# Norm 1's statistics moved to TensorE from a transposed load, and the far lag table made in two halves

## Chip, cores and metric

One core of one Trainium2 chip. The metric is the device time of one execution in microseconds (us), over several executions. Engines: TensorE (PE), VectorE (DVE), ScalarE (ACT), GpSimd (POOL), SyncE (SP, which here only issues transfers).

## The reference, cut to what matters

```python
x = A_u                                                  # 2048 tokens x 512 channels, bf16
h  = x + _A_ref(_layernorm(x), A_re, ..., Dskip)         # "norm 1", then a long convolution over the tokens
h2 = h + _B_ref(_layernorm(h), w1, b1, w2, b2)           # "norm 2", then an MLP over the tokens

def _layernorm(x, axis=-1, eps=1e-5):
    m = jnp.mean(x, axis=axis, keepdims=True)
    v = jnp.var(x, axis=axis, keepdims=True)
    return (x - m) / jnp.sqrt(v + eps)
# _A_ref: K[d,l] = Re sum_n C B dt exp(dt A l);  y = irfft(rfft(u) * rfft(K)) + u * Dskip
# _B_ref: y = gelu(h^T w1 + b1) w2 + b2, transposed back    (w1: 2048 x 1792, w2: 1792 x 2048)
```

## The kernel before

The tokens are 16 blocks of 128. Within a block the convolution is a 128-point transform (`UF`, times the kernel's spectrum `kf`, back through `inv1`, `inv2`). What reaches from earlier blocks goes through "moments" `ms` of the blocks, a shifted copy of them through a scratch in DRAM (`Mb`), a far lag table `G`, and small products `O`. The first half of the tokens (`hf` 0) needs the same as the second (1). The finished blocks `X` are normed (`H`) and multiplied with W1; columns of W1 are either accumulated while the blocks come out, or done afterwards in pairs by a seven-product (Strassen-like) scheme.

```python
    def ln1(self, hf):                                   # statistics of norm 1
        for k in range(lo, hi):
            if k < hi - na:                              # NA = (0, 4)
                b.bn(self.st1[:, k, :], self.X[:, k, :])                               # DVE
            else:                                                                       # ACT
                b.act(self.junk[:, :], self.X[:, k], AF.Copy, accum_out=self.s1[:, 0, k:k + 1])
                b.act(self.cb[:, 0], self.X[:, k], AF.Square, accum_out=self.s1[:, 1, k:k + 1])
        # ... small steps to rs = 1/sigma; Fs = dft * rs; WL = lwin * rs   (cut)
    def shifted(self, hf):                               # ms -> DRAM -> Mb
        self.msw.append(b.dma(self.msd.ap()[120 + 64 * hf:184 + 64 * hf, :], self.ms[64 * hf:64 * hf + 64, :], eng=eng))
        src = bass.AP(tensor=self.msd, offset=64 * hf * D, ap=[[D, P], [8 * D, 8], [1, D]])
        b.dma(self.Mb[:, 8 * hf:8 * hf + 8], src, eng=eng, after=self.msw)
    def lag(self, hf):                                   # far products, 128 per half
        # ... b.mm(self.ps[32 * q:32 * q + 32, 32 * s:32 * s + 32], Gv[:, q, s], Mv[:, q, s])   (cut)
    def y_chunk(self, k):                                # one block out
        # per four blocks, on DVE: Pb = UF * kf(0), UF = UF * kf(1)
        mm(self.bank(yb), self.tb("inv1"), self.Pb[:, t % 2, q], start=True, stop=False)
        mm(self.bank(yb), self.tb("inv2"), self.UF[:, k], start=False, stop=False)
        for f in range(4):                               # the far part
            mm(..., self.tb("lrep", P * f, P), self.O[:, k]...)                         # (cut)
        b.stt(self.X[:, k], self.bank(yb), 1.0, self.X[:, k], ALU.mult, ALU.add, accum_out=self.s2[:, 0, k:k + 1])
    def rest(self):
        first = {0: 3, 1: 6, 2: 7}                       # W1 columns accumulated as blocks come out
        second = {3: 0, 4: 1, 5: 2}                      # (six in all; four pairs by seven products after)
```

A list scheduler sets each engine's order at build time from modelled durations and priorities. A last pass keeps PE warm: wherever its model has PE idle, it fills the gap with products of a constant tile, `ps<-idf`.

```python
    def fill(self):
            # t: when PE is free by the model; start[i]: when the next real product starts by the model
            unit, part = (215.0, 0.92) if cold else (111.0, 0.88)        # ns, share of the gap
            if free and start[i] > t + 60:
                for _ in range(int(part * (start[i] - t - 60) / unit)):
                    ...                                                   # one warming product
```

## Time and profile before

| | before |
|---|---|
| time, median of 2 runs | 156.07 us (155.69 to 156.46) |
| profiled span, granted clock | 154.7 us, 1.000 |
| PE / DVE / ACT busy | 143.5 / 131.4 / 78.2 us |
| last product for `T` (kernel samples) starts on DVE | 34.36 us |
| first lag products (first half of tokens) start | 44.57 us |
| second lag products start (called T_M) | 54.44 us |

Windows: busy time of PE, PEld, DVE, ACT and POOL (with the instructions), the granted clock, the DMA share and GB/s.

```profile
44.57:54.44 9.87, 8.36 (x169) 5.57 (x169) 9.59 (x21) 8.08 (x21) 0.00 (x0) 1.00 0.51 175
54.44:152.40 97.96, 97.55 (x896) 75.13 (x900) 83.02 (x204) 29.86 (x85) 0.00 (x0) 1.00 0.26 96
```

DVE works 9.59 of the 9.87 us before T_M. From T_M to PE's end PE is idle 0.41 us.

### The profile page before, as it was taken

The page shows a single profiled execution, that of the slowest core. Times are in us where ns is not written, and L with a number is a line of the kernel's source. Part 1 is how long each engine was busy: PE and PEld are TensorE (multiplying, and loading weights), DVE is VectorE, ACT ScalarE, POOL GpSimd, SP SyncE. Part 2 cuts the span into 40 slices and gives each one's busy share as a digit, 9 for nine tenths or more (in the row PEclk, how much of TensorE's full clock was granted, in tenths as well). Part 3 has the DMA queues.
Part 4 walks back from the last instruction along what each step waited for, and adds up shares of the span by engine and source line. Part 5 has one row for each costly group of instructions (what it writes and reads, how often), then busy time and mean ns, then how long its engine had stood idle before and what let it go on. Part 6 is the DMA issues. An engine that isn't in the chain of part 4 may idle for free.

```text
span 154.7 us, 3685 instructions
## 1 busy us (share of the span) xinstructions
PE 143.5 (93%) x1522; PEld 106.7 (69%) x1529; DVE 131.4 (85%) x308; ACT 78.2 (51%) x192; POOL 6.7 (4%) x11
## 2 busy tenths in 40 slices
PE   7849869989998889999999999999999999999993
PEld 3738753568565485545554788888888888888882
DVE  5099999998999998999999999957999994558663
ACT  4897999998997868614544832545320000000000
POOL 1590000000000000000000000000000000000000
PEclk9999999999999999999999999999999999999999
DMA  4899996266992508995590000000000101211123
GB/s 108 264 310 360 406 403 240 65 230 176 417 372 83 202 4 310 419 408 222 166 375 3 0 6 0 0 0 4 0 0 0 38 34 68 71 54 51 66 73 103
DMA packets 12351, 23.64 MB, mean 153 GB/s; under 512 B 1181, under 2 KB 8350, under 8 KB 12206
## 3 DMA queue, kind: packets, MB, share of 16 engines
q1 hardware_dynamic: 12190, 23.27, 41.8%
q8 instruction: 12, 0.20, 0.5%
q10 hardware_dynamic: 144, 0.13, 0.2%
q14 instruction: 5, 0.04, 0.1%
HBM read 21.17 MB, written 2.35 MB: 152 GB/s over the span
## 4 chain that ended last, share of the span: by engine, by line
PE 67%; DMA 14%; DVE 7%; SPq 5%; ACT 3%; issue 2%
PE ps L499 67%; DMA tab<-tables 8%; SPq L556 5%; DMA Mb<-ms_scratch 4%; DVE T L522 3%; DVE cmu L522 3%; DMA ms_scratch<-ms 2%; ACT G L506 1%; DVE ct L522 1%; ACT UF L506 1%; PE ps L784 1%; ACT ms L506 0%; ACT kf L506 0%; DVE X L536 0%; ACT mb L506 0%
## 5 line engine op out<-in xcount | busy, mean ns | idle before, releaser
L499 PE MATMUL ps<-H,W 128*128 128x512 bf16 (+1 forms) x180 | 32.5, 327 | 0.3 <-issue 0.2
L499 PEld LDWEIGHTS ps<-H,W 128*128 128x128 bf16 x184 | 17.7, 98 | 10.6 <-DVE H L532 0.2
L784 PE MATMUL ps<-idf 128*128 128x256 bf16 x162 | 22.0, 282 | 1.0 <-POOL idf L547 1.0
L499 PE MATMUL ps<-gT,W 128*128 128x256 bf16 x182 | 22.6, 273 | 0.0
L499 PEld LDWEIGHTS ps<-gT,W 128*128 128x128 bf16 x182 | 17.0, 98 | 3.0 <-DVE X L522 0.2
L784 PEld LDWEIGHTS ps<-idf 128*128 128x128 bf16 x162 | 15.6, 101 | 4.3 <-POOL idf L547 1.0
L522 DVE TENSOR_TENSOR W<-W 128x1024 bf16<-128x1024 bf16 (+1 forms) x23 | 14.9, 657 | 0.3 <-PE ps L499 0.2
L522 DVE TENSOR_TENSOR X<-ps,acc 128x256 bf16<-128x256 f32 x24 | 10.0, 422 | 5.5 <-PE ps L499 5.2
L499 PE MATMUL ps<-HT,W 128*128 128x256 bf16 x112 | 14.2, 273 | 0.0
L506 ACT ACTIVATE H<-X 128x512 bf16<-128x512 bf16 x16 | 10.0, 624 | 7.7 <-DVE X L536 7.7
L536 DVE SCALAR_TENSOR_TENSOR acc<-ps,b2T,X 128x256 f32<-128x256 f32 x24 | 11.1, 481 | 2.8 <-PE ps L499 2.2
L499 PEld LDWEIGHTS ps<-HT,W 128*128 128x128 bf16 x112 | 10.9, 98 | 1.4
L499 PE MATMUL ps<-TS,S 128*128 128x256 bf16 x84 | 11.6, 273 | 0.0
L499 PE MATMUL ps<-TS,W 128*128 128x256 bf16 x84 | 11.3, 273 | 0.0
L536 DVE SCALAR_TENSOR_TENSOR X<-ps,X 128x512 bf16<-128x512 f32 x16 | 10.6, 687 | 0.2 <-PE ps L499 0.2
L506 ACT ACTIVATE gT<-snap,b1T 128x256 bf16<-128x256 f32 x12 | 6.0, 505 | 9.1 <-DVE snap L522 9.1
L542 DVE BATCH_NORM_STATS2 st<-X 128x6 f32<-128x512 bf16 x12 | 7.4, 679 | 3.5 <-DMA X<-in_A_u_dram 3.5
L506 ACT ACTIVATE UF<-ps,ub 128x512 bf16<-128x512 f32 x16 | 10.2, 686 | 0.2 <-PE ps L499 0.2
L499 PEld LDWEIGHTS ps<-TS,S 128*128 128x128 bf16 x84 | 7.9, 98 | 1.4 <-DVE acc L536 0.4
L499 PEld LDWEIGHTS ps<-TS,W 128*128 128x128 bf16 x84 | 8.2, 98 | 1.0
L506 ACT ACTIVATE gT<-ps,b1T 128x512 bf16<-128x512 f32 (+1 forms) x10 | 5.4, 606 | 4.7 <-PE ps L499 4.7
L499 PEld LDWEIGHTS ps<-O,tab 128*128 128x128 bf16 x64 | 4.8, 98 | 3.9 <-DVE O L530 0.8
(127 smaller groups left out, 233.4 us busy)
## 6 DMA issues: line engine op xcount, KB each, us to landing
W<-in_B_w_dram SPq DMA_DIRECT2D x4, 1792.0 KB, 10.9
W<-in_B_w_dram SPq DMA_DIRECT2D x2, 2048.0 KB, 9.3
W<-in_B_w_dram SPq DMA_DIRECT2D x2, 1536.0 KB, 7.9
Mb<-ms_scratch SPq DMA_DIRECT2D x2, 1024.0 KB, 6.0
out_dram<-X SPq DMA_DIRECT2D x15, 128.0 KB, 1.7
tab<-tables SPq DMA_DIRECT2D x1, 1296.0 KB, 13.1
X<-in_A_u_dram SPq DMA_DIRECT2D x4, 256.0 KB, 4.7
X<-in_A_u_dram SPq DMA_DIRECT2D x2, 512.0 KB, 11.8
```

The costliest lines, as they stand in the source:

```text
L499: return self.r.add("pe", lambda e: e.matmul(out, lhsT=lhsT, rhs=rhs, start=start, stop=stop, skip_group_check=onto), [lhsT, rhs], [out], ...
L506: return self.r.add("act", lambda e: e.activation(out=out, in_=in_, func=func, bias=bias, scale=scale, accum_out=accum_out), [in_, bias, s ...
L522: return self.r.add(eng, lambda e: e.tensor_tensor(out=out, in0=a, in1=b, op=op), [a, b], [out], self._d(eng, nel(out), m), **k)
L536: return self.r.add(eng, lambda e: e.scalar_tensor_tensor(out=out, in0=a, scalar=s, in1=b, op0=op0, op1=op1, accum_out=accum_out), [a, s, ...
L542: return self.r.add("dve", lambda e: e.bn_stats(out=out, in_=a), [a], [out], 67 + nel(a) / 0.96, **k)
L556: return self.r.add(eng, lambda e: e.dma_start(out=out, in_=in_), [in_], [out], max(by / RATE.get(out.tensor.name.split("_")[0], 410) + 0. ...
L784: self.rec.hot = (hot, lambda e, bk: e.matmul(self.bank(bk, 0, 256), lhsT=hv[:, 0:P], rhs=hv[:, :], start=True, stop=True))
```

## The change

The intent: take norm 1's statistics off DVE and ACT. x is loaded a second time, transposed by the DMA (`XT`, channels on partitions); PE multiplies 32 tokens by themselves, so that the diagonal of each 32x32 block holds the sums of squares, and by a column of ones for the sums. DVE only masks out the diagonal and adds. The far table is made in two halves of its columns, so that the first lag products can start when half of it is there. W1's loads go behind the shifted copies, the copy of the second half is split, four W1 columns instead of six are accumulated and five pairs instead of four done by seven products. All priorities were set anew. Not in the diff shown: the blocks come out through four banks of PSUM (the accumulators that PE writes) instead of two, the evictions of the table, of `kf` and of `O` are divided otherwise between DVE and ACT, and a quarter of W2 is loaded later.

```diff
-        for i in range(3):
-            ld(17 + i, self.X[:, 2 * i + 2:2 * i + 4], xv[:, 2 * i + 2:2 * i + 4])
-        # ... two more loads of X  (cut)
+        for h in range(2):
+            ld(17 + h, self.XT[:, h], self.x_in[0][L // 2 * h:L // 2 * h + L // 2], transpose=True)
+            ld(8 + h, self.X[:, 8 * h:8 * h + 8], xv[:, 8 * h:8 * h + 8])
-        for q in range(2):
-            ld(13 + q, self.W1[:, 4 * q:4 * q + 4], w1v[:, 4 * q:4 * q + 4])
+        self.w1q = lambda *qs: [ld(13 + q, ..., after=self.msw) for q in qs]      # (cut)
+    def stats(self, hf):
+        for k in range(8):                                                        # section gm0 / gm1
+            for c in range(4):
+                for q in range(4):
+                    t = XT[:, c, P * k + 32 * q:P * k + 32 * q + 32]
+                    b.mm(self.bank(bk, 32 * k, 32 * k + 32, 32 * q, 32 * q + 32), t, t, start=c == 0, stop=c == 3, onto=True)
+        for k in range(8):
+            for c in range(4):
+                b.mm(self.bank(bk, 256 + k, 257 + k), XT[:, c, P * k:P * k + P], self.ones, ...)
+        b.tt(self.gd[:, :, :], self.bank(bk, 0, 256)..., self.mk32..., ALU.mult)  # then a tensor_reduce
     def shifted(self, hf):
+        if hf:
+            self.shift_rows(1, 0, 64)                     # the half of the copy that needs only the first moments
+        self.shift_rows(hf, 64 * hf, P - 64 * hf)
+        self.w1q(*((1, 2, 3) if hf else (0,)))
     def far(self):
+        for h in range(2):                                # halves of columns: kt[rows, h] -> G[:, h]   (cut)
-        first = {0: 3, 1: 6, 2: 7}
-        second = {3: 0, 4: 1, 5: 2}
+        first = {0: 2, 1: 3, 2: 0, 3: 1}
+        second = {}
+PAIRS = [(6, 10), (7, 11), (8, 12), (9, 13), (4, 5)]
```

## The prediction

> **What bounds the kernel now.** I read the chain that ended last first. In order of time (start, length, what):
>
> ```profile
> 33.76 3.49 PE ps L499 x126
> ...
> 44.22 0.70 ACT ms L506
> ...
> 44.93 3.14 DMA ms_scratch<-ms
> ...
> 48.09 6.31 DMA Mb<-ms_scratch
> ...
> 54.44 2.85 PE ps L499 x114
> ```
>
> Up to 33.8 us VectorE (DVE) prepares the kernel samples; then samples, tables, the moments `ms` of the second half of the tokens, their way through DRAM into `Mb`, and from 54.44 us TensorE (PE) alone to 152.3 us. The windows show how full PE then is:
>
> ```profile
> 60.00:70.00 10.00, 9.95 (x58) 5.05 (x58) 9.77 (x25) 4.39 (x16) 0.00 (x0) 1.00 1.02 414
> 90.00:100.00 10.00, 10.00 (x94) 8.89 (x92) 9.49 (x25) 3.52 (x10) 0.00 (x0) 1.00 0.01 2
> ```
>
> 94 products of 256 columns in 10 us are 0.107 us each: nothing to squeeze but the number of columns. The time is thus "when does the second `Mb` land" (T_M = 54.44) plus the PE work still undone then. The timelines of DVE and ScalarE (ACT) show what precedes T_M (start, length, [idle before]):
>
> ```profile
> 7.55 4.85 DVE L542 BATCH_NORM_STATS2 st<-X 128x6 f32<-128x512 bf16 x8 [3.50 <-DMA X<-in_A_u_dram]
> 12.31 0.41 DVE L522 TENSOR_TENSOR m<-EX,CX 128x512 bf16<-128x512 bf16 x1
> ...
> 34.36 0.81 DVE L522 TENSOR_TENSOR T<-E,SC 128x1280 bf16<-128x1280 bf16 x1
> 35.10 1.87 DVE L542 BATCH_NORM_STATS2 st<-X 128x6 f32<-128x512 bf16 x3
> ```
> ```profile
> 7.84 1.28 ACT L512 ACT_TABLE_LOAD   x1
> 9.13 0.72 ACT L506 ACTIVATE CX<-AW,cst 128x512 bf16<-128x512 f32 x1
> ```
>
> DVE is full from 7.55 to 35.1 us. But the eight statistics instructions stand where DVE would wait for ACT anyway: the first sine (`CX`) is only ready at 9.8 us.
>
> **What the Trainium skill says.** (1) "DMA: Bandwidth & Descriptors", Latency and other measured facts: a DMA transpose reached 261 GB/s with a non-contiguous middle dimension, about 350 to 400 if contiguous. No run here shows one; plain loads here run at 264 to 417 GB/s. (2) "TensorE: Matmul & The Clock Gate", Wait — 56ns, not 53.3ns?: small products start no closer than about 25 ns. The trace has 128 products `ps<-Mb,G` of 32 columns in 2.86 us, 22 ns each: agrees roughly, and I use 22. (3) Same page, The HAM clock gate: after an idle window of about 3.4 us the array falls to half clock. The trace agrees at the start: the first ten warming products take 2.32 us (0.23 each), forty later ones 4.54 us (0.11).
>
> **The change, part by part.**
>
> *Statistics.* Removed: 12 statistics instructions on DVE (7.3 us at 0.61 pace: eight take 4.85) and on ACT eight passes with accumulators (8 x (0.62+0.19), about 6 us). Added on PE: per half 128 products of 32x32 (2.8 us) and 32 of one column (about 0.9, at the 28 ns of `ps<-cmu,T`), where PE now only warms itself. Added on DVE: per half a masked product, a sum, two small ones, about 1.0 us.
>
> *Loads.* 2 MB of transposed x are added ahead of the table; W1 moves behind the shifted copies. In queue order: parameters 0.8 MB, transposed half 1 MB, x half 1 MB, table 1.3 MB, second transposed half 1 MB. Estimate at 300 GB/s for plain loads and the skill's 261: first half lands near 11 us, table 18, second half 21. The statistics end near 16 and 26 us on PE.
>
> *The walk to T_M in the new order*, with the paces of the old trace. ACT starts the sines 0.6 us earlier (one square moved) and CX is ready at 9.2. DVE then runs, in the new program's order: level products up to SN done at 18.6; `rden` arrives 18.9; first statistics and a wait for ACT's four exponentials to 21; Fs to 24.6; then two T products and small ones 26.5; second statistics 27.3; T 28; `cmu` 31.7; three T 33.9; second WL and Fs 35.3 (before, this came after T); last two T 36.8. The sum: 25.3 us busy and about 1.9 idle from 9.2, against 22.8 us busy from 12.31 before. So the last T comes 1.7 us **later** than at 35.1: the gain at the front is 3.1 us, and 1.9 us of waits, 2.0 of new statistics and 1.5 of Fs moved ahead (less 0.6 of small ones) eat it.
>
> From there: samples `g` end 38.7 (62 products of 28 ns after the last T); evicted 39.5; `phi` first (40.0), then selection (41.1), `kt` 41.7. DVE does kf and the 2.3 us pair of spectrum products before its two G evictions (0.57 each): the first half of the far table is ready at 44.1. The halves do help: before, all of G ended at 43.9 although `kt` came 2 us earlier. First lag products at 44.3; the second moments stand behind 32 of them: `ms` done near 47.2 (before 44.92). Write 3 us as before; the read is now half as large (the other half goes early), 4 us instead of 6.3, an estimate from 2 us fixed and 0.5 MB at 250 GB/s. T_M' is about 54.2: unchanged.
>
> *PE work after T_M.* Before, six token blocks of the inverse transform were done by then (each 4 x 0.054 + 2 x 0.216 = 0.65); in the new order the lag products of the second half stand ahead of all the last steps of those blocks, so only eight of their products (1.7 us) are done: +2.2 us. One pair of W1 blocks more by the seven-product scheme: 32 x 0.216 become 56 x 0.107: -0.9 us. Net +1.3.
>
> *A DVE-bound stretch.* Only four column blocks of W1 instead of six are accumulated while the blocks come out: 4 x 0.216 + 0.65 = 1.5 us of PE per block instead of 1.95. DVE needs per block 0.61 (eviction), 0.33 (norm), 0.33 (differences), and in four batches 2.27 of spectrum products, plus 2.4 for the new W1 sums placed in the middle: about 28 us to the last norm, and it can begin only 2 us after T_M'. Walking the two orders against each other, PE waits 0.45 (first norm), 1.0 (block 13, behind the spectrum products), 1.3 (block 15, behind the W1 sums), 0.95 and 0.55 (norms 6 and 7): 4.3 us, where before it waited some 0.6.
>
> **Sum.** 54.2 - 54.44 + 1.3 + 4.3 - 0.6 is +4.8 us: about 160.8 from 156.07. Since waits inside a tuned order tend to overlap, I shade it to 159.8.
>
> **Rivals.** (a) *The old statistics were on the path.* All of the 7.3 us off DVE and 6 off ACT comes through, T_M' falls to 50 or less, the stretch starts earlier and the total is 151 to 153. For it: DVE is full up to 35 us and the chain runs over it from 21.9; and somebody set all priorities anew. Against: eight of the twelve stand in a wait for ACT, four after the last T. (b) *Even.* The second half of x arrives as I think, the read of half `Mb` is quick (3 us), and DVE's stretch overlaps better: 154 to 158. For it: the seven-product saving of 0.9 is certain and the errors of my walk are 1 to 2 us. (c) *The transposing DMA is slow* (half of 261 GB/s, or long to issue): second half near 29 us, DVE waits in the middle for it, everything is 5 to 7 us later: 165 or more. Nothing in the old trace speaks for or against. (d) *Half clock* after PE's wait of some 3 us before T_M': 1 to 2 us more, mostly inside the DVE-bound waits.
>
> **Range and chances.** Errors of the walk to T_M' about 1.2 us, of the waits about 2, the transpose a tail upward, rival (a) a tail downward: 154.2 to 164.5. Faster means below 152.9, which needs (a); slower means above 159.2, just under the centre.
>
> **What would show each step.** Right: the DVE timeline has the last T at 36 to 37.5 us; `ms` of the second half ends after 46; the lag products of the second half start at 53 to 55.5 with PE idle before them on DMA `Mb`; then PE idle of 3 to 5 us up to 90 us, released by DVE X and H; the later windows unchanged at 94 products in 10 us. Wrong: the last T below 34, or second lag products before 51 us (then (a)); PE dense after T_M' (then even); `ps<-XT` waiting for DMA beyond 26 us (then (c)).

## More of the kernel before

One thing more matters for what follows: what the engines do while the second `Mb` is on its way.

The timeline of DVE of the kernel before (start, length, what) shows with what it fills the wait: finished blocks of `X`, four of them before T_M, the first at

```profile
50.11 0.69 DVE L536 SCALAR_TENSOR_TENSOR X<-ps,X 128x512 bf16<-128x512 f32 x1
...
53.15 1.22 DVE L522 TENSOR_TENSOR Pb<-UF,kf 128x2048 bf16<-128x2048 bf16 x1
```

## The result, and the profile after

After: 166.38 us, median of 2 runs (165.71 to 167.06), clocks 0.969 and 0.979; before: 156.07. The ratio of fast runs is 1.0661 with a 95% interval of 1.0443 to 1.0879: slower. A ratio is the mean time of one kernel's fast runs over that of the other's of the same rounds, so not quite the ratio of the medians quoted. The result is correct.

The chain that ended last, of the kernel after (start, length, what), in answer to that of before:

```profile
18.40 0.50 PE ps L501 x13
18.91 9.26 PE ps L786 x61
28.16 2.20 PE ps L501 x162
30.39 0.43 DVE gd L524
...
39.50 1.48 DVE T L524 x2
...
50.67 0.69 ACT ms L508
51.38 1.95 DMA ms_scratch<-ms
53.35 4.72 DMA Mb<-ms_scratch
58.11 3.94 PE ps L501 x90
```

The end of the chain has the predicted shape: last `T`, `ms`, write, read, second lag products. But each of these is about 4 us later than predicted, and the front of the chain is new: L786 is the warming product. 61 of them, 9.26 us, stand in front of the second statistics (`x162`), which DVE then takes up (`gd`). The timeline of PE of the kernel after, at that place, has the idle time before each group in brackets:

```profile
12.26 1.20 PE L501 MATMUL ps<-XT 128*32 128x32 bf16 x128
13.39 0.63 PE L501 MATMUL ps<-idf,XT 128*128 128x1 bf16 x19
18.40 0.50 PE L501 MATMUL ps<-idf,XT 128*128 128x1 bf16 x13 [4.39 <-issue]
18.77 9.39 PE L786 MATMUL ps<-idf 128*128 128x256 bf16 x61
28.09 0.38 PE L501 MATMUL ps<-XT 128*32 128x32 bf16 x32
```

PE stops for 4.39 us in the middle of the first statistics, waiting for nothing that the profile shows (what it is follows under plain_load). Then the 61 warming products take 9.3 us, 0.154 each instead of 0.111 in the scheduler's model, because the granted clock was 0.55 from 17.9 to 24.7 us. The second half of `XT` had landed at 23.7. DVE waits for the second statistics (its timeline, kernel after), and is idle twice more while `Mb` is on its way:

```profile
25.68 0.82 DVE L524 TENSOR_TENSOR T<-E,SC 128x1280 bf16<-128x1280 bf16 x1
30.39 0.42 DVE L524 TENSOR_TENSOR gd<-ps,mk 128x256 f32<-128x256 f32 x1 [3.89 <-PE ps L501]
...
54.96 1.23 DVE L524 TENSOR_TENSOR Pb<-UF,kf 128x2048 bf16<-128x2048 bf16 x1 [2.88 <-ACT UF L508]
56.22 1.23 DVE L524 TENSOR_TENSOR UF<-UF,kf 128x2048 bf16<-128x2048 bf16 x1
60.51 0.69 DVE L538 SCALAR_TENSOR_TENSOR X<-ps,X 128x512 bf16<-128x512 f32 x1 [3.06 <-PE ps L501]
```

The first block comes out at 60.51, 2.4 us after T_M; before it was 50.11, 4.3 us ahead of T_M. Windows of the kernel after, in answer to those of before:

```profile
48.89:58.11 9.22, 7.57 (x166) 4.19 (x164) 5.61 (x6) 7.81 (x19) 0.00 (x0) 1.00 0.45 107
58.11:163.10 104.99, 100.72 (x948) 79.93 (x952) 89.24 (x221) 34.61 (x102) 0.00 (x0) 0.98 0.37 139
100.00:110.00 10.00, 10.00 (x94) 8.96 (x92) 8.55 (x18) 3.43 (x9) 0.00 (x0) 1.00 0.09 34
```

So the 10.7 us split in two. T_M is 3.67 later (58.11 against 54.44). From T_M to PE's end it takes 104.99 instead of 97.96, 7.03 more: 3.17 of it as busy time of PE, 3.86 as idle time. The late windows are as dense as before, 94 products in 10 us. Most of the idle time is five waits, all for DVE (timeline of PE, kernel after):

```profile
72.19 0.39 PE L501 MATMUL ps<-Pb,tab 128*128 128x512 bf16 x1 [0.50 <-DVE X L538]
77.35 0.39 PE L501 MATMUL ps<-Pb,tab 128*128 128x512 bf16 x1 [1.29 <-DVE X L538]
79.02 2.30 PE L501 MATMUL ps<-H,W 128*128 128x256 bf16 x14 [0.84 <-DVE X L538]
81.53 2.76 PE L501 MATMUL ps<-H,W 128*128 128x512 bf16 x12 [0.22 <-DVE H L534]
86.17 5.26 PE L501 MATMUL ps<-H,W 128*128 128x256 bf16 x27 [0.79 <-DVE H L534]
```

They sum to 3.64 us. And the transposing loads hold SP's queue (timeline of SP, kernel after; the length is that of issuing, not of landing):

```profile
4.09 4.16 SPq L551 DMA_TRANSPOSE XT<-in_A_u_dram  x1
8.30 0.57 SPq L558 DMA_DIRECT2D X<-in_A_u_dram  x1
...
10.01 10.07 SPq L551 DMA_TRANSPOSE XT<-in_A_u_dram  x1
```

The ordinary load of the same megabyte takes 0.57. The two transposed halves land 6.3 and 13.7 us after their issue began, at 10.4 and 23.7.

### The profile page after: what moved, and what is told of

It is laid out like the page before. It is cut to its first block, busy times and chain, and to the rows that moved or that the text cites.

```text
span 165.3 us, 4321 instructions
## 1 busy us (share of the span) xinstructions
PE 149.0 (90%) x1851; PEld 113.3 (69%) x1860; DVE 129.3 (78%) x299; ACT 75.6 (46%) x183; POOL 6.7 (4%) x11
## 3 DMA queue, kind: packets, MB, share of 16 engines
q1 hardware_dynamic: 20398, 25.37, 47.2%
## 4 chain that ended last, share of the span: by engine, by line
PE 55%; DVE 28%; DMA 6%; issue 4%; POOL 3%; ACT 1%; SPq 1%; POOLq 1%
PE ps L501 48%; PE ps L786 7%; DVE X L538 4%; DVE S L524 3%; DMA Mb<-ms_scratch 3%; DVE T L524 3%; DVE W L524 3%; DVE H L534 2%; DVE acc L538 2%; POOL bc L524 2%; DVE HT L524 2%; DMA raw<-in_A_C_re_dram 2%; DVE cmu L524 1%; DMA ms_scratch<-ms 1%; DVE V L524 1%
## 5 line engine op out<-in xcount | busy, mean ns | idle before, releaser
L501 PE MATMUL ps<-H,W 128*128 128x256 bf16 (+1 forms) x166 | 28.3, 313 | 1.9 <-DVE H L534 1.0
L786 PE MATMUL ps<-idf 128*128 128x256 bf16 x141 | 22.7, 316 | 1.1 <-POOL idf L546 1.0
L501 PE MATMUL ps<-gT,W 128*128 128x256 bf16 x182 | 23.3, 273 | 0.1
L501 PEld LDWEIGHTS ps<-H,W 128*128 128x128 bf16 x168 | 15.8, 98 | 10.2 <-DVE H L534 1.8
L786 PEld LDWEIGHTS ps<-idf 128*128 128x128 bf16 x141 | 15.0, 113 | 5.2 <-POOL idf L546 1.0
L501 PE MATMUL ps<-HT,W 128*128 128x256 bf16 x128 | 15.6, 273 | 0.0
L501 PEld LDWEIGHTS ps<-HT,W 128*128 128x128 bf16 x128 | 12.4, 98 | 1.5
L508 ACT ACTIVATE gT<-snap,b1T 128x256 bf16<-128x256 f32 x15 | 7.0, 502 | 6.5 <-DVE snap L524 6.4
L508 ACT ACTIVATE snap<-ps 128x256 f32<-128x256 f32 x15 | 5.5, 380 | 9.4 <-PE ps L501 9.3
L501 PE MATMUL ps<-Mb,G 128*32 128x32 bf16 x256 | 6.2, 256 | 1.5 <-DMA Mb<-ms_scratch 1.0
L501 PEld LDWEIGHTS ps<-Mb,G 128*32 128x32 bf16 x256 | 5.4, 174 | 2.8 <-issue 1.5
```

The source lines that it names most:

```text
L501: return self.r.add("pe", lambda e: e.matmul(out, lhsT=lhsT, rhs=rhs, start=start, stop=stop, skip_group_check=onto), [lhsT, rhs], [out], ...
L508: return self.r.add("act", lambda e: e.activation(out=out, in_=in_, func=func, bias=bias, scale=scale, accum_out=accum_out), [in_, bias, s ...
L786: self.rec.hot = (hot, lambda e, bk: e.matmul(self.bank(bk, 0, 256), lhsT=hv[:, 0:P], rhs=hv[:, :], start=True, stop=True))
```

## The experiments

Where an experiment needed another order of instructions, the list scheduler's choice was replaced by a list of sections for each engine; such an order is told in words. All results are correct except plain_load's. A run is called slow when it is over 1.5% above the fastest of the same kernel; ratios use fast runs alone.

| profile of | T_M: second lag products start | first block out on DVE | last norm done | last `X` on DVE | last `X` minus last norm |
|---|---|---|---|---|---|
| before | 54.44 | 50.11 | 82.60 | 152.82 | 70.22 |
| after | 58.11 | 60.51 | 87.62 | 163.46 | 75.84 |
| half_warming | 55.98 | 58.39 | 85.77 | 161.61 | 75.84 |
| warm_gap | 54.78 | 56.74 | 84.75 | 160.59 | 75.84 |
| old_stats | 54.69 | 56.68 | 84.69 | 160.88 | 76.19 |
| y_first | 57.85 | 57.54 | 86.40 | 162.24 | 75.84 |
| y_sooner | 58.92 | 54.97 | 86.07 | 161.91 | 75.84 |
| y_sooner_hw | 55.22 | 51.51 | 83.01 | 158.85 | 75.84 |
| y_sooner_w1 | 56.91 | 53.20 | 82.26 | 158.10 | 75.84 |
| w1_early_y | 54.03 | 54.34 | 81.12 | 157.32 | 76.20 |
| old_w1 | 59.36 | 58.26 | 92.53 | 165.42 | 72.89 |

(From the timelines of PE and DVE; "last norm" is the end of the last `H<-X,sm`, "last `X`" the end of the last instruction that writes `X`.) The last norms of the kernels before and after:

```profile
82.19 0.41 DVE L532 TENSOR_SCALAR H<-X,sm 128x512 bf16<-128x512 bf16 x1
86.89 0.73 DVE L534 TENSOR_SCALAR H<-X,sm 128x512 bf16<-128x512 bf16 x2
```

After the last norm PE is full, so the last column is the PE work still left then. It does not depend on T_M or on the order: it is about 76 wherever four W1 columns were accumulated and five pairs left, 70.2 in the kernel before with six and four.

**First question: what holds up T_M?** My theory was the warming products and the stall that stand in PE's order ahead of the second statistics; the rival, the transposing loads themselves.

*no_warming*: the warming products ahead of the second statistics left out.

```diff
-            if free and start[i] > t + 60:
+            if free and start[i] > t + 60 and not ops[i].sec.startswith('gm1'):
```

> The changed kernel without the 61 warming products that stand between the two halves' statistics on TensorE; nothing else differs. Theory A (after the 4.4 us issue stall TensorE falls to half clock, and the warming products, sized for a full clock, then take 9.4 us and stand in order ahead of the second statistics): the first products of the second half start as soon as its transposed x has landed, near 23.7 us instead of 28.1; DVE's wait of 3.9 us before gd falls below 1; T_M (start of the lag products of the second half) falls from 58.1 to about 54 to 55 and the time by 3 to 4 us, to 162.5-163.5. Rival B (the second transposed half itself lands near 28 us): no start before 28, time unchanged within 0.7 us.

166.03 us, ratio 1.0584 (1.0515 to 1.0653). The profile (clock 0.918) is used here only for the order of events. Its timeline of PE:

```profile
18.11 0.51 PE L501 MATMUL ps<-idf,XT 128*128 128x1 bf16 x13 [4.36 <-issue]
24.08 0.41 PE L501 MATMUL ps<-XT 128*32 128x32 bf16 x32 [5.46 <-DMA XT<-in_A_u_dram]
...
50.80 1.04 PE L501 MATMUL ps<-X,WL 128*32 128x512 bf16 x4 [2.13 <-issue]
```

The second statistics now wait for the data and start at 24.08, 4.0 us earlier; the last `T` is at 36.32. But PE, idle for 5.46 us, is cold afterwards (granted clock 0.50 from 24 to 30 us; its fast runs too have a lower mean clock, 0.938 to 0.948, than the kernel after's 0.969 and 0.979), and it stalls again ("issue") at 41.5 and 48.7, so little arrives at the end. The warming products are both the delay and what they are there for.

*half_warming*: the same place, half as many (30 instead of 61).

```diff
-                for _ in range(int(part * (start[i] - t - 60) / unit)):
+                for _ in range(int(part * (start[i] - t - 60) / unit / (2 if ops[i].sec.startswith('gm1') else 1))):
```

> The changed kernel with 30 instead of 61 warming products ahead of the second half's statistics, and no other edit: the missing step of the prediction taken alone. If that queue is why T_M came at 58.1 instead of the predicted 54.2: second statistics from about 24 us, the last T done at 37 (predicted 36.8), lag products from 45 (predicted 44.3), T_M 54 to 55, the first eviction near 57, and, with DVE's work and the rest after it as before (102.5 us), the last X instruction at 159 to 160 against 162.98; time 162.5-164. If only half of it comes through (TensorE cold, as in no_warming): 165.

164.66 us, ratio 1.050 (1.0435 to 1.0566). The profile's span is 163.5, of the kernel after 165.3, at the same clock (0.969). By the ratios alone the two are not told apart, since the kernel after has only two runs; by the traces they are. PE, and then DVE, of half_warming:

```profile
18.47 5.09 PE L786 MATMUL ps<-idf 128*128 128x256 bf16 x30
24.55 0.38 PE L501 MATMUL ps<-XT 128*32 128x32 bf16 x32 [0.99 <-DMA XT<-in_A_u_dram]
```
```profile
26.93 0.42 DVE L524 TENSOR_TENSOR gd<-ps,mk 128x256 f32<-128x256 f32 x1 [0.52 <-PE ps L501]
...
36.69 0.81 DVE L524 TENSOR_TENSOR T<-E,SC 128x1280 bf16<-128x1280 bf16 x1
```

With 31 warming products fewer DVE's wait falls from 3.89 to 0.52, the last `T` starts at 36.69 and is done at 37.50 (the prediction said 36.8), and T_M is 55.98. Of the 3.67 us that T_M was late, 2.1 are gone, and 1.85 of them reach the end (161.61 against 163.46). The time of 164.66 is just above the expected 162.5 to 164. The same edit to another order of the kernel (y_sooner and y_sooner_hw, below) takes 3.7 us off T_M and brings 1.4 in the medians; there the runs of the two do not overlap (164.70 to 166.98, and 162.48 to 164.48).

*plain_load*: the transposed loads replaced by ordinary ones of the same size (wrong result, relative error 0.054).

```diff
-            ld(17 + h, self.XT[:, h], self.x_in[0][...], transpose=True)
+            ld(17 + h, self.XT[:, h], self.x_in[0][...].rearrange("(p c) d -> p (c d)", p=P)...)
```

> The changed kernel with the two crossbar loads of x made ordinary loads of the same bytes (the result is wrong on purpose: the statistics are of the wrong elements). Theory A (the transposes hold the issuing queue and the DMA engines, and TensorE's instruction fetch with them): no issue stall of 4.4 us at 14 us, the second load is issued by 10 us in under 1 us and lands before 20, the second statistics start at 22 us or earlier (then bounded by the warming products), time 4 to 5 us less, about 162. Rival C (the stall comes from the number of small products that TensorE has to fetch): the stall of about 4 us stays, and the time with it.

165.2 us, ratio 1.0555 (1.0484 to 1.0625), span 163.0. SP's queue and PE of plain_load:

```profile
4.06 0.43 SPq L558 DMA_DIRECT2D XT<-in_A_u_dram  x1
```
```profile
16.33 0.32 PE L501 MATMUL ps<-idf,XT 128*128 128x1 bf16 x6 [2.80 <-issue]
```

Issuing falls from 4.16 and 10.07 us to 0.43 and 0.45. The stall of PE falls from 4.39 to 2.80 but stays. The scheduler, which knows the transfers' modelled times, chose another order, with a wait of DVE for ACT of 3.75 us at 25.3, so the total says little about the transposes. What follows is only that the stall of PE does not need them.

What the stall is: the instructions themselves come by DMA, in packets of 16,384 bytes. The profile shows their number (packets, MB, share; kernel after, then before):

```profile
q8 instruction: 14, 0.23, 0.6%
q8 instruction: 12, 0.20, 0.5%
```

The packed traces have the time of each packet, and PE's instructions (products and weight loads) can be counted in them up to each stop. In the sixteen traces (three are slow and serve for the order only) there are 19 stops of over 0.5 us that wait for "issue". In each, PE resumes 1.28 to 1.59 us after such a packet has landed; in the kernel after the packet is on its way from 16.05 to 17.12 us and PE resumes at 18.40. And the stops stand at fixed places: in all ten kernels with the new statistics the first comes after exactly 449 instructions, three others after 705, and the rest after 1215, 1467 to 1473 (three), 1729 and 1985. That is 449 and then multiples of 256 more, to within 6 (some records can be missing). So PE had used up its instructions and waited for the next packet. Nor did the packet come later than it does with the old loads: in the six kernels with the old statistics the first packet lands at 16.30 to 17.34, in nine of those with the new ones at 16.20 to 17.23 (plain_load 14.98). But with the old statistics PE has started only 168 to 193 instructions by 14.0 us and reaches the 450th after 30 us, while the new ones have used up 449: 128 tiny products, of two instructions each, are gone in 1.2 us. No run changed the number of instructions alone, and what sets the time at which a packet comes is not shown.

**Second question: is T_M what sets the time?** My rival theory: even with T_M as before, the change is slower.

*old_stats*: loads, statistics and the order of the front as before; halves of the table, copies, W1 scheme and the rest as in the change. (Edit: the old `bn`, `ln_small`, `ln1` and `loads` put back, except W1's.)

> The changed kernel with the statistics, their loads and the order of the front part taken back to the kernel before (12 on DVE, 8 passes on ACT, no transposed x); the halved far table, the W1 block and everything behind it keep the changed kernel's order. If the front part lost 4.3 us and the rest of the change 6.3: last T near 35, first lag products at 44.5 to 45.5, T_M 53 to 54, time about 161.5 to 162.5. If most of the loss is in the statistics through effects further on: 158 or less. If the new statistics are innocent: 165 or more.

164.96 us, ratio 1.0543 (1.0472 to 1.0615); granted clock in the profile 1.000. Its window from T_M:

```profile
54.69:160.50 105.81, 100.32 (x948) 79.32 (x952) 89.24 (x221) 34.56 (x102) 0.00 (x0) 1.00 0.36 137
```

T_M is that of the kernel before, to 0.25 us, and the time from there is 105.81 instead of 97.96. The new statistics are not needed at all for most of the loss.

*warm_gap*: half_warming with 12 warming products ahead of the second lag products, against the half clock after the wait for `Mb` (0.59 granted from 58.11 to 62.30 us in the kernel after).

```diff
+            gap = ops[i].sec == "O1.0:pe" and ops[i] is next(p for p in ops if p.sec == "O1.0:pe")
-                for _ in range(int(...)):
+                for _ in range(12 if gap else int(...)):
```

> half_warming with 12 warming products more, directly ahead of the lag products of the second half, where TensorE waits about 1 us for the copies and the clock is then granted at half for 3.4 us. The products after it (16 of 128 columns, 1.89 us there against 1.06 at full clock) stand ahead of the first eviction: at full clock the first eviction and the end come 0.5 to 1 us earlier than in half_warming. If the 12 products delay the lag products by as much as they save: no difference.

164.69 us, ratio 1.0507 (1.0424 to 1.0589): the same as half_warming. The half clock is gone (1.00 in the window from T_M), but in the profiled run another stall of PE took its place:

```profile
58.69 0.47 PE L504 MATMUL ps<-Mb,G 128*32 128x32 bf16 x14 [1.06 <-issue]
```
```profile
54.78:160.70 105.92, 100.55 (x952) 79.29 (x952) 89.62 (x221) 34.25 (x100) 0.00 (x0) 1.00 0.36 137
```

Here too T_M is within 0.4 us of the kernel before, now with the new statistics. PE's last product ends at 160.07, so 105.3 us follow (this window was taken 0.6 us too long). Four traces with T_M from 54.69 to 58.11 (after, half_warming, warm_gap and old_stats) need 104.8 to 105.7 us from there to PE's end. Up to T_M the program of warm_gap is that of half_warming but for the 12 products; that its T_M is 1.2 us earlier (54.78 against 55.98) shows how far two single profiles can differ.

**Third question: what makes it 105 instead of 98?** Candidates: DVE begins to take blocks out only after T_M; W1's sums lie in the DVE-bound stretch because W1 is loaded late; the choice of four columns and five pairs.

*y_first*: order only; the last steps of blocks 0 to 3 ahead of the second lag products.

> The changed kernel with one reordering only: the lag products of the first half all run before the inverse-transform blocks, and the last steps of blocks 0 to 3 run before the lag products of the second half, so that DVE can take out four blocks in its 2.9 and 3.1 us of idle time at 52 to 60.5 us. Theory D (what is lost after T_M is that DVE, the bound from 50 to 94 us, starts its evictions some 4 us late): the first X eviction near 57 instead of 60.5, TensorE's waits for DVE X and H between 66 and 94 us fall from 4 to about 1, half clock at 58.8 us gone or shorter; time 3 to 4 us less, about 163. Rival E (those waits are set by DVE's own amount of work in the stretch, above all the W1 sums placed in it, or by having only four column blocks): waits stay near 4 and the time falls by less than 1.5.

165.94 us, ratio 1.0594 (1.054 to 1.0649). The first block comes out at 57.54 instead of 60.51, but behind DVE's spectrum products, for which it has waited 3.9 us for ACT's `UF`, and it waits 1.2 us more at 61.3. The last norm gains 1.2. Little.

*y_sooner*: order only; the blocks interleaved so that each comes out as soon as its spectrum is there, and the third pair of spectrum products behind the first four blocks.

> The changed kernel with the order alone altered: all lag products of the first half directly after the moments, then the token blocks 1, 3, 0, 2 (and 5, 7) finished ahead of the lag products of the second half, and DVE takes these blocks out before the spectrum products of blocks 8 to 11. A pattern in the nine traces so far: the last X instruction of DVE comes 101.7 to 104.2 us after its first eviction of a token block (kernel before 50.11 and 152.34; changed kernel 60.51 and 162.98), whatever T_M does; old_w1, whose evictions are in pieces, is the exception. Theory G (the time is the first eviction plus about 102.5): the first eviction comes near 55 us instead of 60.5, T_M stays at 57 to 58, and the time falls by 4 to 5 us, to 161-162.5. Rival (T_M plus the TensorE work left is what counts, as the prediction has it): T_M is unchanged and five blocks' last steps are moved ahead of it, 1 us of work: 165 to 166. y_first, a weaker version in which DVE did the spectrum products first, gave 165.94.

165.67 us, ratio 1.0551 (1.0456 to 1.0646). The first block is out 5.54 us earlier, the last norm only 1.55. This refutes the simple form of the theory, that the end moves with the first block: DVE's spectrum products (2.45 us) and 1.2 us more of idling now lie behind it.

*y_sooner_hw*: y_sooner with the 30 warming products of half_warming.

> y_sooner with 30 warming products instead of 61 ahead of the second half's statistics. If the front loss is the warming products standing in order before the statistics: the second statistics start near 24 us instead of 28, DVE's last T comes at 36.3 to 37 instead of 40.2, the lag products start near 45.5 to 46 and the first eviction near 52; time 2.5 to 4 us under y_sooner. If TensorE gets cold through it and its products of samples and tables take twice as long (as in no_warming, where 4 us at the last T became 1.5 at the lag products): 1 us or less.

164.27 us, ratio 1.0427 (1.0349 to 1.0505). DVE's last `T` is at 36.20, its first block at 51.51, near the kernel before's 50.11, the last norm at 83.01, 0.4 behind it. In this trace, then, DVE's time is made up. The last `X` is still 6.0 us later, and 5.62 of that is the last column of the table: the work left for PE.

*w1_early*: old_stats with W1 loaded as before, and the first of W1's sums at 48 us, where DVE idled.

```diff
-        self.w1q = lambda *qs: [ld(13 + q, ..., after=self.msw) for q in qs]
+        w1q = lambda *qs: [ld(13 + q, ...) for q in qs]
+        w1q(0, 1)                                        # and self.late = lambda: w1q(2, 3), as before
```

> The run old_stats with two things more taken back: the four W1 loads stand where the kernel before has them (two early, two near 35 us, not behind the shifted copies), and so the 2.4 us of W1 sums for the first seven-product pair can stand in DVE's idle time near 48 us instead of in the middle of the evictions at 71 us. In old_stats DVE is idle 2.8, 2.7 and 1.4 us between 48.6 and 60.6 and then over 96% busy up to 90. Theory F (the loss after T_M is DVE work pushed out of that idle time into the stretch where DVE is the bound, because W1 comes late): TensorE's waits of 0.50, 1.29, 0.84, 0.22 and 0.78 us shrink to about half, time 2 to 3 us under old_stats (164.96), so 162-163. Rival E2 (DVE starts its evictions too late and the position of the sums does not matter): less than 1 us.

164.83 us; ratio 1.0454 (1.0351 to 1.0557), from two fast runs, 163.30 and 163.78. The profile is slow, with a stall of 1.57 us at 37.4; it is not used.

*w1_early_y*: the same with y_first's order.

> w1_early with the order of y_first as well: blocks 0 to 3 are finished ahead of the lag products of the second half, so DVE's first eviction comes near 54 to 55 us instead of 56.7 (kernel before: 50.1). If both pushed-out pieces add up: 4 to 6 us under old_stats, about 159-161. If the first eviction is all that counts: the same 2 us under w1_early. If neither: equal to old_stats within 1 us.

162.13 us, ratio 1.0369 (1.029 to 1.0448). *y_sooner_w1*: the same with y_sooner's order.

> w1_early_y (old statistics, early W1) with the order of y_sooner. Theory G: the first eviction comes near 51 us (it was 54.34 there, behind the spectrum products), so the time is 3 us less: 158-159.5 against 162.13; that is within 1 to 2% of the kernel before, with the halved far table and the five pairs still in. Rival (DVE's amount of work in the stretch is what counts, not its start): 161 or more.

162.39 us, ratio of the two fast runs (160.33 and 161.70) 1.0245 (1.015 to 1.0341): whether it is over 2% is unclear, but it is slower than before. In both traces the last norm is no later than in the kernel before (81.12 and 82.26 against 82.60). The end is still 4.5 and 5.3 us later.

*old_w1*: the change with W1's old scheme, six columns accumulated and four pairs (`first`, `second`, rings and buffers of before).

> The changed kernel with the kernel before's scheme for W1: six column blocks accumulated and four seven-product pairs instead of four and five, y in two banks, the old priorities of that part; statistics, transposed x, halved far table and loads as changed. TensorE then has 1.95 us of work per token block instead of 1.5, so DVE's 28 us no longer bound the stretch: waits for DVE X and H between 62 and 90 us fall from 3.9 to about 1, one pair less costs 0.9. Theory: time 1.5 to 3 us less than the changed kernel, 163.5-165. If the four-column scheme is not what exposes the waits: 166 or more.

168.42 us, ratio 1.0771 (1.0698 to 1.0843): worse than the change. The work left after the last norm falls to 72.89, but six columns need all banks, so blocks go through two banks again, and DVE waits 5.8 us for its first block and 2.6 soon after; the last norm is at 92.53. In the change's order the old scheme does not fit. The run does not show the new scheme to be a mistake in itself. As I read it, it goes with a stretch in which PE has to wait for DVE anyway, and pays for it later; no run isolates this.

*before_halves*: the kernel before with the table's halves and the split copy.

> The kernel before with only the far lag table in two halves of columns and the shifted copies of the second half of the tokens split in two, and nothing else of the change (order held as close to the kernel before as the halves allow). The lag products start at about 41.5 to 42 us instead of 44.6 and the second copies land 1 to 2 us earlier. If the start of the lag products or T_M is what the end follows: 153.5 to 154.5. If DVE, full from 39 to 90 us in the kernel before, is what it follows: no change, 155.5-157, as DVE's work is the same.

160.15 us over four runs, of which one was fast, at 157.36, against a median before of 155.94. No ratio can be had from that. It shows no gain from the halves, and does not settle whether they cost.

*all_mended*: y_sooner_hw with W1 loaded ahead of the shifted copies, so that its sums can be done early.

```diff
+        self.w1q(0, 1, 2, 3)                             # right after params()
-        self.w1q(*((1, 2, 3) if hf else (0,)))
```

> y_sooner_hw (new statistics, 30 warming products, blocks finished early) with the W1 loads no longer behind the shifted copies: two quarters right after x (near 23 us), two when the last T is done (near 37 us), and the W1 sums of the first extra pair (2.4 us on DVE) in DVE's idle time ahead of the first evictions. An identity read from the 13 traces so far: DVE's last X instruction = first eviction + DVE's busy time from there to the last norm + its idle time there + 75.4 us (75.36 to 75.73 in ten traces with the changed W1 scheme; 69.74 and 69.75 in the two with the scheme of before; old_w1 72.4). Here: first eviction near 51.5, busy 26.6 (29.06 less 2.4), idle about 2, so the last X instruction at 155.5 against 158.4 in y_sooner_hw and 152.3 in the kernel before; time 2 to 3.5 us under y_sooner_hw (164.27 median), 161-162.5. Rival: the W1 quarters in flight delay the moments' copies, T_M comes at 56 or later and the time is not below y_sooner_hw.

169.81 us, ratio 1.0869 (1.0794 to 1.0943), the slowest of all. SP's queue, and DVE, of all_mended:

```profile
48.02 0.48 SPq L565 DMA_DIRECT2D ms_scratch<-ms  x1
59.05 0.60 SPq L565 DMA_DIRECT2D Mb<-ms_scratch  x1
```
```profile
58.84 0.69 DVE L531 TENSOR_TENSOR V<-W 128x1024 bf16<-128x1024 bf16 x1 [10.68 <-DMA W<-in_B_w_dram]
```

The read of `Mb` can be issued only when the write of `ms` has landed, and that took until 59.05 behind W1's data, 11.0 us instead of 1.95. In the change, x is loaded twice and the transposes hold the queue until 20.1 us; W1, of which two quarters were here issued at 41 us, ahead of the second copies, then blocks them. Whether another place in the queue would have let its sums be done early was not tried.

No variant beat the kernel before.

## Why the prediction was wrong, point by point

The direction was right, the time was outside the range: 166.38 against 159.8 and at most 164.5. By its own steps:

- **What bounds the kernel** (T_M plus the PE work left): held for one order behind T_M. In four kernels with T_M from 54.69 to 58.11 the time from T_M to PE's end stayed within 0.9 us. Where that order was altered (y_first, y_sooner, y_sooner_hw, y_sooner_w1, w1_early_y) it was 100.7 to 103.9: T_M alone does not set the end, and y_sooner has a later T_M than the kernel after and an earlier end.
- **Where the statistics went** ("eight of the twelve stand in a wait for ACT, four after the last T", so little gain): right. Rival (a) did not happen: in no kernel with the new statistics is the last `T` ahead of the kernel before's 34.36 (the earliest starts at 36.16).
- **"The statistics end near 16 and 26 us on PE", and with them the walk to the last `T` done at 36.8 and T_M' = 54.2**: this is the step that failed. Measured: first statistics end 18.9, second 30.3, last `T` done 40.96, T_M 58.11, 3.9 us over. The walk followed DVE and the transfers and took PE as free, since there it "only warms itself". But PE stopped for 4.39 us, because its own instructions had not come; it fell to half clock; and 61 warming products stood in its order ahead of the second statistics. None of the three was in the walk. The products alone would not have done it: with the first statistics done at 14.5 and 0.11 each they would have ended near 21 us (an estimate), ahead of the data at 23.7. They began 4.4 us late and ran at 0.154. That DVE's part of the walk was nearly right is shown by half_warming: last `T` done at 37.50 (the prediction's own sum, 25.3 us busy and 1.9 idle from 9.2, ends at 36.4, not 36.8).
- **First lag products at 44.3, `ms` 47.2, write 3, read 4**: measured 48.9, 51.4 (its end), 1.95, 4.72. Late by the same 4 us; write and read together 6.7 instead of 7.
- **PE work after T_M, +1.3**: the count of products in the two orders, with the records that the traces miss, gives +1.24, so the work is right. But PE's busy time grew by 3.17. About 0.8 is the half clock of rival (d), 58.11 to 62.30: half_warming, which has it too, is busy for 101.39 us from T_M, warm_gap, without it, for 100.55. Each wait also shows its last product 0.38 us long instead of 0.22, which is seven times 0.16, 1.1 us, as an estimate. I had neither in the sum.
- **PE waits 0.45, 1.0, 1.3, 0.95 and 0.55, together 4.3**: measured 0.50, 1.29, 0.84, 0.22 and 0.79, together 3.64. Right in cause and nearly in size; so was "28 us to the last norm", from 2 us after T_M: measured 27.1 from 60.51.
- **The shading of 1 us downwards** because waits overlap: wrong. PE's idle time grew by 3.86, against 3.7 (4.3 less 0.6) in the sum before the shading.
- **Rival (c)**, slow or long to issue: true in part. The issue took 4.16 and 10.07 us, and the second half landed at 23.7 instead of 21, but DVE's wait for it (3.89) was for PE's warming products, not for the transfer.

The sum, measured: 3.9 for T_M, 1.9 for PE's busy time, 0.2 for idle time (3.86 against 4.3 less 0.6), together 6.0 over the unshaded 160.8; the medians differ from it by 5.6.

Where the gain hoped for went: the statistics' 7.3 us of DVE and 6 of ACT were mostly off the path already. Even in half_warming the last `T` is done 2.3 us later than in the kernel before (37.50 against 35.17). And with x loaded twice W1 was put behind the copies, so that its sums fell into the stretch after T_M.

What stays open: what sets the time at which PE's instruction packets come (in plain_load the first landed 1.2 us or more earlier than in the others, and the stop was 1.6 us shorter than the kernel after's); and, in warm_gap, up to 0.8 us of PE's busy time after T_M, which grew by 3.00 there (1.24 by count, about 1.0 by the tails of six waits). Stops of this kind of 1 to 2 us also appeared at other places in no_warming, w1_early and warm_gap, so differences of 1 us between single profiles here should not be trusted.

## What to carry to other kernels

Instructions that only fill a gap are in the order too: when data comes earlier than the model thinks, or the filler runs at half clock, they are the delay, so cost them like work before you believe a walk. A burst of tiny products can use up PE's instructions faster than they come: count them. Ask of an engine's relief whether the work stood in a wait; if it did, taking it away moves only the wait. And when a transfer is added in front, follow what it pushes back in the queue to the engine that will have to make up for it later.

## What the Trainium skill lacked or had wrong

- "Advanced Engine Details and Errata", X-Bar Transpose (TRN2): "TRN2 transpose DMAs are as fast as regular DMAs". Here 1 MB took 6.3 and 13.7 us from issue to landing, 166 and 77 GB/s with all waiting included; the ordinary load of 1 MB in the same kernel 6.4 us (median of two). The first agrees, the second, with the table and x beside it, does not.
- "DMA: Bandwidth & Descriptors", Latency and other measured facts, gives 261 GB/s for a transpose, and Rules for kernel authors says that one next to ordinary transfers "needs nothing". Neither tells what issuing costs: 4.16 and 10.07 us of the issuing queue for 1 MB each, against 0.43 to 0.87 for an ordinary megabyte (kernel after and plain_load), and everything behind it in that queue waits. The "needs nothing" stands where the page speaks of corrupted data, not of time, and its cycle counts for issuing a transpose are for other cases.
- "TensorE: Matmul & The Clock Gate", Wait — 56ns, not 53.3ns?, has a floor of about 25 ns from start to start. The 32x32 statistics in four groups of columns ran 128 in 1.20 us, 9 ns each; I had costed them at 22. The same page's Measured speedup vs the span model has some 4 ns for a further tile, but the lag products, of the same shape and also in four groups, took 22 each (64 in 1.40 us), so what makes the difference is not shown.
- "Runtime: NRT & Kernel Launch", Instruction fetch mechanics, has the instructions fetched in blocks of 256, which the stops 256 apart agree with, but calls the fetch hidden and knows a stall only behind a branch. Here PE stopped without a branch: 4.39 us after 449 instructions, among the last of them 128 tiny products in 1.2 us, until 1.28 us after a packet of 16,384 bytes had landed, and 0.64 to 4.86 us in other traces.
- "TensorE: Matmul & The Clock Gate", The HAM clock gate, agrees: after the stall of 4.39 us the granted clock was 0.55 (17.9 to 24.7 us). In the 61 filling products this made 0.154 us each of the 0.111 planned.
